# Two staging buffers for token-major Q and K, their stores in the sync queue, and turned blocks moved into the next tile

## Chip, cores, metric

One core of one Trainium2 chip. The metric is device microseconds of one execution of the program. A difference is called faster or slower from 2% on, and below that it is given with its interval.

## The reference, cut to what matters

Forward and backward of a small transformer block: a recurrent attention with memory, then a gated FFN. The part that matters here is the forward recurrence over 64 segments of 32 tokens. Each segment attends over 8 memory rows and its own 32 tokens, and its output gives the memory rows of the next segment, so the segments are a chain:

```python
for s in range(n_seg):
    h = concatenate([mem, xs], axis=1)
    q, k, v = h @ Wq, h @ Wk, h @ Wv
    p = softmax(where(mask, q @ k.T * scale, -1e9))
    o = (p @ v) @ Wo
    mem = o[:, :M, :]          # the next segment needs this
    outs.append(o[:, M:, :])
```

The rest (FFN, backward recurrence, weight gradients) comes after the chain and reads what the chain saved: Q and K by token (T1; the T0 blocks hold those of the memory rows), V, the attention output by token (X_o), its projection by rows (Oh), the weights turned, that is transposed on their way by the DMA (Td, To, Tg, Tu, Tq, Tk, Tv).

## The kernel before

A tile is four segments; r is the segment's place in it, jm its place among sixteen. The chain's instructions have a high priority. Everything else in a segment is side work on the sync queue (SP) and on GpSimd (POOL): turned transfers through two staging buffers, and their stores.

```python
qk_st = A(15, 2, 2, 512)                       # one buffer for token-major Q and K
stg_b = [A(36 + 4 * i, 2048) for i in range(2)]  # two staging buffers

def stg():                                     # next staging buffer, in turn
    rot[0] += 1
    for fn in unsaved.pop(rot[0] % 2, ()): fn()   # its last content is stored first
    return stg_b[rot[0] % 2]
def save(*pairs):                              # a store from GpSimd, put off
    ... nc.gpsimd.dma_start(out=out, in_=in_) ...
def piece():                                   # turn one of 44 pieces of weights
    T, ot = dr["T" + nm], stg()
    nc.sync.dma_start_transpose(out=..., in_=Ws[...]); save((T[...], ot))
...
        with k.prio.crit():                    # the chain
            ...
            qk_turned(s, 0)
            for w, nm in enumerate("qk"):
                nc.scalar.dma_start(out=dr["T1" + nm][s], in_=qk_st[:, w]...)
            ...
        nc.gpsimd.dma_start(out=dr["P_all"][s], ...)
        for g in range(2):
            nc.sync.dma_start(out=dr["VG"][s, ...], in_=Vs[...])
        rest_rows(s + 1)                       # GpSimd copies that the next scores need
        nc.gpsimd.tensor_copy(out=mblk[:, :, jm * M:(jm + 1) * M], in_=orr)   # frees orr
        if due and jm % 3 == 0 and jm > 0:
            residual(n, h_t, x2_t, to_v)       # VectorE; rows fetched at jm % 3 == 1
        save_all()
        if r == 1:  ... T0 block: stg, transpose, save
        if r < 3 and s >= 4:
            piece()
        if jm == 15: ... orow = projection of the memory block, stored to Oh
        if r == 3:
            to_token_major(xblk, t, at)        # both halves of a tile, X_o
        if jm == 15:
            to_token_major(mblk, ...)          # two more, and one for mh
```

The tool that builds the program takes the order of each engine's instructions from the data dependencies and its priorities. The order of the text is not the order of issue.

Of the kernel before, what the change touches and what calls it, by code (L numbers as in the profile page):

```python
# [10 lines left out]
BF16 = mybir.dt.bfloat16  # L11
# [4 lines left out]
P = 128  # L16
# [129 lines left out]
def run_all(k: _K):  # L146
    nc, tc, ctx = k.nc, k.tc, k.ctx
    S, D, M, H, Dh, HD, F = k.S, k.D, k.M, k.H, k.Dh, k.HD, k.F
    SEG, L, NSEG, NT, KC, DP, MC, DC, FC = k.SEG, k.L, k.NSEG, k.NT, k.KC, k.DP, k.MC, k.DC, k.FC
# [25 lines left out]
    ident = const.tile([P, P], BF16)  # L175
# [28 lines left out]
    def dt(name, shape, dtype=BF16):  # L204
        return dram.tile(shape, dtype, name=name)
# [3 lines left out]
    dr = dict(XN=dt("XN", [NB * P, DP]), Hh=dt("Hh", [S, D]), HN=dt("HN", [S, D]), DH=dt("DH", [S, D], FP32),  # L209
              DHb=dt("DHb", [NB * P, DP]), Zt=dt("Zt", [S, F]), DGP=dt("DGP", [S, F]), DU=dt("DU", [S, F]),  # L210
              VG=dt("VG", [NSEG, 2 * L, W2]), XR=dt("XR", [NT * 32, DP]), P_all=dt("P_all", [NSEG, P, 8 * L]),
              X_o=dt("X_o", [NB, P, MC * P]), HC=dt("HC", [NB * P, DP]), Oh=dt("Oh", [S, D]))
# [2 lines left out]
        dr["M_" + nm] = dt("M_" + nm, [NT, P, MC * 32])  # L215
    for nm in ("q", "k", "v"):
        dr["T" + nm] = dt("T" + nm, [P, MC, D])
    for nm in ("q", "k"):
        dr["T1" + nm] = dt("T1" + nm, [NSEG, P, 1024])
        dr["T0" + nm] = dt("T0" + nm, [NSEG // 8, P, W2])  # L220
    dr["To"] = dt("To", [P, KC, HD])
    dr["Td"] = dt("Td", [P, KC, F])
# [127 lines left out]
def forward_chain(k: _K):  # L350
    nc, tc = k.nc, k.tc
    S, D, M, H, Dh, HD = k.S, k.D, k.M, k.H, k.Dh, k.HD
    SEG, L, NSEG, NT, KC, DP, MC, DC = k.SEG, k.L, k.NSEG, k.NT, k.KC, k.DP, k.MC, k.DC
    X2 = k.aps["A_x"][0]
    MEM0 = k.aps["A_mem0"][0]
    ident, dr, sel, maskb = k.ident, k.dr, k.sel, k.maskb
    smal = k._small
    W, A, B = k.W, k.A, k.B
# [5 lines left out]
    HB = 4  # L364
    qT_b = [A(2.5 * i, 32, L) for i in range(2)]
    kT_b = [A(5 + 2.5 * i, 32, L) for i in range(2)]
    V_b = [A(11, 2048), W(92, 2048)]
    qk_st = A(15, 2, 2, 512)
    hR_b = [A(19 + 0.5 * i, KC, 64) for i in range(2)]
    R_b = [[W(56 + 4 * i, 32, 64) for i in range(2)], [A(20 + 4 * i, 32, 64) for i in range(2)]]  # L370
    stg_b = [A(36 + 4 * i, 2048) for i in range(2)]
    xblk_b = [A(52 - 24 * i, 32, P) for i in range(2)]
    mblk = A(44, 32, P)
# [4 lines left out]
    or_b = [B(1.25 + 0.5 * i, 32, M) for i in range(3)]  # L378
    x2_t, h_t = B(2.75, D), B(3.625, D)
    hx = B(4.5, KC, P)  # L380
    orow = B(6.25, D)
    P_b = [B(7.125 + 0.625 * i, 8, L) for i in range(2)]
    mh = B(8.375, KC, P)
    om_b = [B(9.375 + 0.5 * i, 256) for i in range(2)]
    maskt = B(10.375, HB * L)

    nc.gpsimd.memset(hT_flat[:, :, NWIN * L:], 0.0)
    nc.gpsimd.memset(PT_bd, 0.0)
    om = k.f32("f1", 256, "om")
    pO = k.po1()  # L390
    nc.vector.memset(pO[:], 0.0)
    nc.vector.tensor_copy(out=maskt.rearrange("p (h n) -> p h n", n=L), in_=maskb[:].unsqueeze(1).to_broadcast([P, HB, L]))
# [101 lines left out]
    def stg():  # L494
        rot[0] += 1
        for fn in unsaved.pop(rot[0] % 2, ()):
            fn()
        return stg_b[rot[0] % 2]

    def save(*pairs):  # L500
        def fn():
            for out, in_ in pairs:
                nc.gpsimd.dma_start(out=out, in_=in_)
        unsaved[rot[0] % 2] = [fn]

    def save_all():
        for i in (1, 2):
            for fn in unsaved.pop((rot[0] + i) % 2, ()):
                fn()
# [5 lines left out]
    def qk_rows(s, b):  # L515
        sl = s % NWIN
        banks = [k.ps1(), k.ps1()]
        for w in range(2):
            for kc in range(KC - 1):
                for q in range(4):  # L520
                    nc.tensor.matmul(banks[w][32 * q:32 * q + 32, :], lhsT=hT_roll[:, kc, sl, M:L], rhs=(Wq_sb, Wk_sb)[w][:, kc, col(q, b)],  # L521
                                     start=(kc == 0), stop=False, skip_group_check=True)
        for q in range(4):
            for w in range(2):
                last = nc.tensor.matmul(banks[w][32 * q:32 * q + 32, :], lhsT=hT_roll[64 * w:64 * w + 64, KC - 1, sl, M:L],
                                        rhs=Wqk3[64 * w:64 * w + 64, col(q, b)], start=False, stop=True, skip_group_check=True)
        for w in range(2):
            k.evac(qk_st[:, w, b, :], banks[w][:], "vs"[w])
        return last

    def qk_turned(s, b):
        pt = k.ps1()[:].bitcast(BF16)
        for w in range(2):
            for i in range(4):
                nc.tensor.transpose(pt[:, w * 512 + i * P:w * 512 + (i + 1) * P], qk_st[:, w, b, i * P:(i + 1) * P], ident[:, :])
        for w, dst in ((0, qT_b[s % 2]), (1, kT_b[s % 2])):
            k.evac(dst[:, 16 * b:16 * b + 16, M:L], pt[:, w * 512:(w + 1) * 512].rearrange("p (c n) -> p c n", n=32), "vs"[w])

    def to_token_major(blk, t, ins=None):
        for hf in range(2):  # L540
            ot = stg()
            with tc.issue_after(ins) if ins is not None else nullcontext():
                nc.sync.dma_start_transpose(out=ot.rearrange("p (a b) -> p a b", b=P),
                                            in_=blk[:, 16 * hf:16 * hf + 16, :].rearrange("p c n -> p (c n)"))
            save((dr["X_o"][t][:, hf * 2048:(hf + 1) * 2048], ot))

    pieces = []
    for nm, Ws in (("d", k.aps["B_w_down"]), ("o", k.Wo2)):
# [6 lines left out]
    def piece():  # L555
        if not pieces:
            return
        nm, Ws, i0, n = pieces.pop(0)
        T, ot = dr["T" + nm], stg()
        if nm in "do":  # L560
            o4 = ot.rearrange("p (c n) -> p c n", c=KC)
            nc.sync.dma_start_transpose(out=o4[:, 0:3, 0:n], in_=Ws[i0:i0 + n, 0:3 * P])
            nc.sync.dma_start_transpose(out=o4[:, 3, 0:n], in_=Ws[i0:i0 + n, D - P:D])
            save((T[:, 0:3, i0:i0 + n], o4[:, 0:3, 0:n]), (T[0:64, 3, i0:i0 + n], o4[64:P, 3, 0:n]))
        else:
            m = n // P
            o3 = ot[:, 0:m * D].rearrange("p (c d) -> p c d", d=D)
            nc.sync.dma_start_transpose(out=o3, in_=Ws[:, i0:i0 + n])
            save((T[:, i0 // P:i0 // P + m, :], o3))
# [18 lines left out]
    for s in range(NSEG):  # L588
        t, r = divmod(s, 4)
        jm = s % 16  # L590
# [3 lines left out]
        xblk, om2 = xblk_b[t % 2], om_b[s % 2]  # L594
        end = s == NSEG - 1
        if due and jm % 3 == 1:
            fetch(due[0], h_t, x2_t)
        with k.prio.crit():
# [86 lines left out]
                k.fl.at(0)  # L685
                k.fl.at(1)
            qk_turned(s, 0)
            for w, nm in enumerate("qk"):
                nc.scalar.dma_start(out=dr["T1" + nm][s], in_=qk_st[:, w].rearrange("p b n -> p (b n)"))
            value_rows(0)  # L690
            pS0 = scores(0)
            softmax(0, pS0)
# [34 lines left out]
        nc.gpsimd.dma_start(out=oh[s, M:SEG, 0:256], in_=om2[0:24, :])  # L727
        nc.gpsimd.dma_start(out=oh[s, M:SEG, 256:D], in_=om2[32:56, 0:D - 256])
        nc.gpsimd.dma_start(out=dr["P_all"][s], in_=P_sb.rearrange("p h n -> p (h n)"))
        for g in range(2):  # L730
            nc.sync.dma_start(out=dr["VG"][s, L * g:L * g + L], in_=Vs[64 * g:64 * g + L, :])
        if not end:
# [7 lines left out]
        if due and jm % 3 == 0 and jm > 0:  # L740
            n = due.pop(0)
            residual(n, h_t, x2_t, to_v)
        save_all()
        if (r == 0 and t > 0) or s == 2:
            prep_tile(t + 2)
        if r == 1:
            w = bu // 4
            ot = stg()
            nc.sync.dma_start_transpose(out=ot.rearrange("p (a b) -> p a b", b=P), in_=R_b[bm % 2][w].rearrange("p c n -> p (c n)"))
            save((dr["T0" + "qk"[w]][bm], ot))  # L750
        if r < 3 and s >= 4:
            piece()
        at = None
        if jm == 15:
            px = k.fx1()
# [4 lines left out]
            due = list(range(t - 3, t + 1))  # L760
            if end:
                at = k.fl.at(3).ins
        if r == 3:
            to_token_major(xblk, t, at)
        if jm == 15:
            to_token_major(mblk, NT + s // 16, at)
            mrow = stg()
            nc.sync.dma_start_transpose(out=mrow[:, 0:DP].rearrange("p (a b) -> p a b", b=P),
                                        in_=mh.rearrange("p c n -> p (c n)"))
            r0 = (NT + s // 16) * P  # L770
            save((dr["XN"][r0:r0 + P, :], mrow[:, 0:DP]))
    save_all()
    assert not pieces and due == list(range(NT - 4, NT))
    late = [(B(0, D), B(0.875, D)), (W(61.5, D), W(62.375, D))]
# [178 lines left out]
def backward_chain(k: _K):  # L953
    nc, tc = k.nc, k.tc
# [37 lines left out]
    def load_seg(s):  # L992
        if s < NSEG - 1:
            load_v(s)
        for nm, T_sb in (("q", Q_sb), ("k", K_sb)):
            t1 = dr["T1" + nm][s].rearrange("(g x i) n -> g i x n", g=2, x=2)
            t0 = dr["T0" + nm][s // 8].rearrange("(x s i) (g n) -> s g i x n", x=2, s=8, g=2)
            for g in range(2):
                for src, i0, i1 in ((t1[g], M, L), (t0[s % 8, g], 0, M)):
                    nc.sync.dma_start(out=T_sb[64 * g + i0:64 * g + i1].rearrange("p (x c) n -> p x (c n)", x=2), in_=src)  # L1000
        P_sb = Pb[s % 2]
        nc.gpsimd.dma_start(out=P_sb.rearrange("p h n -> p (h n)"), in_=dr["P_all"][s])
        for g in range(2):
            pool_op = nc.gpsimd.tensor_copy(out=P_bd[64 * g:64 * g + L, :, g, :], in_=P_sb[64 * g:64 * g + L, :, :])
        stores("mid", s, pool_op.ins)
# [419 lines left out]
```

## Time and profile before

| | before |
|---|---|
| median | 3188.19 us (four runs, 3183.85 to 3195.59; 3185.03 of three at the time of the prediction) |
| span of the profiled run | 3196.7 us, mean granted clock 0.974 (an execution of 3198.43 us, not among the four) |
| forward chain, end of segment 0 to end of segment 62 | 998.4 us |
| a clean segment | 15.09 us |

A segment's end is the end of the VectorE copy that writes the next memory rows. A segment's length is the difference of two such ends, so lengths can be compared one by one between kernels. In the views PE is TensorE, PEld its weight loads, DVE VectorE, ACT ScalarE, POOL GpSimd; a q at the end (SPq, ACTq) marks issues of transfers in that engine's queue. arA, arB and arW are on-chip buffers, psf, po and fx the accumulators that matmuls write; the chain's copies out of them are called evictions. One more view: GpSimd's timeline at the end of segment 19. The columns are the start, the time, engine, line, operation, tiles, count and, in brackets, the idle time before and what ended it.

```profile
374.52 0.51 POOL L727 DMA_DIRECT2D Oh<-arB  x1 [4.32 <-DVE arB L713]
375.02 1.08 POOL L739 COPY arA<-arB 128x256 bf16<-128x256 bf16 x3
376.05 0.56 POOL L759 DMA_DIRECT2D Oh<-arB  x1
...
379.66 0.55 POOL L503 DMA_DIRECT2D X_o<-arA  x1 [2.00 <-DMA arA<-arA]
```

### The profile page before, as it was taken

What the parts mean: (1) busy time and instruction counts of PE and PEld (TensorE: products, weight loads), DVE (VectorE), ACT (ScalarE), POOL (GpSimd) and SP (SyncE); (2) the same over time, 40 slices, a digit from 0 to 9 for tenths busy, and PEclk for the clock granted to TensorE, in tenths of its full rate; (3) what the DMA queues carried; (4) which work ended last, traced back from release to release, by engine and by line L of the source; (5) the groups of instructions that cost most, each with busy time, mean ns of one, the idle gap of its engine ahead of it and who ended that gap; (6) DMA issues with size and microseconds to landing.
All of it is one profiled execution on the core that took longest, in us unless ns stands there. A gap on an engine that the chain in (4) does not pass through costs nothing.

```text
span 3196.7 us, 107765 instructions
## 1 busy us (share of the span) xinstructions
PE 2924.5 (91%) x47442; PEld 1776.2 (56%) x47442; DVE 1364.9 (43%) x3433; ACT 1057.8 (33%) x2501; POOL 723.7 (23%) x1648
## 2 busy tenths in 40 slices
PE   6899899989988869977999999999999699999998
PEld 3455455555544547645666666666666454444444
DVE  4455455455455567753444544445444201111110
ACT  2444344344434323322333333333433101110210
POOL 2232332223232221121112211112211111111111
PEclk9999999999999979988999999999999899999999
DMA  6968765867667888894454555445545898959952
GB/s 237 198 152 177 181 163 141 194 162 183 167 155 192 246 207 195 191 274 147 132 138 137 132 149 134 140 132 140 144 134 141 266 269 226 198 181 195 191 147 72
DMA packets 757305, 556.21 MB, mean 174 GB/s; under 512 B 627732, under 2 KB 656388, under 8 KB 754404
## 3 DMA queue, kind: packets, MB, share of 16 engines
q1 hardware_dynamic: 671828, 294.81, 44.2%
q0 software_dynamic: 66576, 220.95, 20.3%
q10 hardware_dynamic: 18432, 33.56, 3.1%
q8 instruction: 372, 6.09, 0.8%
q14 instruction: 97, 0.79, 0.1%
HBM read 167.32 MB, written 234.23 MB: 126 GB/s over the span
## 4 chain that ended last, share of the span: by engine, by line
PE 69%; DMA 10%; DVE 9%; issue 7%; ACT 3%; SPq 2%; POOL 1%; ACTq 0%; POOLq 0%; DVEq 0%
PE psf L1286 8%; PE po L1120 7%; PE psf L1071 7%; PE psf L633 5%; PE psf L521 4%; PE psf L1048 4%; PE psf L1307 4%; PE po L678 3%; PE fx L1184 3%; PE psf L847 2%; DVE arA L75 2%; PE fx L454 2%; PE fx L937 2%; PE fx L1291 2%; PE psf L1142 2%
## 5 line engine op out<-in xcount | busy, mean ns | idle before, releaser
L75 DVE CAST arA<-psf 128x256 bf16<-128x256 f32 (+4 forms) x997 | 470.8, 492 | 920.1 <-PE psf L1286 258.9
L76 ACT CAST arA<-psf 128x384 bf16<-128x384 f32 (+6 forms) x979 | 390.0, 420 | 1179.8 <-PE psf L1286 256.5
L1120 PE MATMUL po<-arW,arA 128*32 128x448 bf16 x6144 | 348.9, 357 | 22.8 <-DVE arA L75 20.5
L633 PE MATMUL psf<-arW,arA 128*64 128x512 bf16 x1536 | 253.3, 393 | 0.0
L1286 PE MATMUL psf<-arW,arA 128*128 128x512 bf16 x1000 | 252.0, 379 | 0.0
L1071 PEld LDWEIGHTS <-arW 128*128 128x128 bf16 x8192 | 214.1, 96 | 27.5 <-issue 27.5
L1120 PEld LDWEIGHTS <-arA 128*32 128x32 bf16 x6144 | 152.1, 97 | 135.9 <-DVE arA L75 21.7
L1286 PEld LDWEIGHTS <-arA 128*128 128x128 bf16 x1440 | 136.0, 98 | 164.8 <-issue 13.8
L1071 PE MATMUL psf<-arA,arW 128*128 128x40 bf16 x8192 | 217.7, 180 | 8.4 <-DVE arA L1146 5.1
L521 PE MATMUL psf<-arW,arA 128*32 128x512 bf16 x3072 | 193.9, 385 | 12.5 <-DVE arA L722 12.5
L847 PE MATMUL psf<-arW 128*128 128x256 bf16 x1344 | 159.3, 281 | 45.1 <-DMA arW<-arW 34.3
L847 PEld LDWEIGHTS <-arW 128*128 128x128 bf16 x1344 | 134.9, 101 | 71.5 <-DMA arW<-arW 29.1
L678 PE MATMUL po<-arW,arA 128*32 128x256 bf16 (+1 forms) x4096 | 142.4, 265 | 9.8 <-DVE arA L75 6.8
L1048 PEld LDWEIGHTS <-arW 128*128 128x128 bf16 x2048 | 87.6, 100 | 89.6 <-issue 62.9
L1048 PE MATMUL psf<-arB,arW 128*128 128x80 bf16 x2048 | 98.1, 202 | 41.4 <-DMA arW<-T0k 22.6
L454 PE MATMUL fx<-arA,arW 128*128 128x64 bf16 (+1 forms) x2048 | 84.8, 196 | 43.2 <-ACT arB L76 30.7
L1081 ACT COPY arA<-psf 128x1024 bf16<-128x1024 bf16 x128 | 123.3, 1015 | 2.3 <-PE psf L1080 0.4
L521 PEld LDWEIGHTS <-arA 128*32 128x32 bf16 x3072 | 70.5, 96 | 90.1 <-DVE arA L722 18.1
L76 ACT COPY arA<-psf 128x512 bf16<-128x512 bf16 (+2 forms) x136 | 79.0, 582 | 111.5 <-DVE arA L75 87.9
L678 PEld LDWEIGHTS <-arA 128*32 128x32 bf16 x4096 | 94.6, 97 | 30.2 <-DVE arA L75 10.2
L633 PEld LDWEIGHTS <-arA 128*64 128x64 bf16 x1536 | 85.0, 111 | 44.1 <-issue 1.4
L454 PEld LDWEIGHTS <-arW 128*128 128x128 bf16 (+1 forms) x2048 | 71.2, 99 | 65.4 <-issue 43.8
(285 smaller groups left out, 4618.6 us busy)
## 6 DMA issues: line engine op xcount, KB each, us to landing
X_o<-arA POOLq DMA_DIRECT2D x40, 512.0 KB, 4.1
T1k<-arA ACTq DMA_DIRECT2D x64, 256.0 KB
T1q<-arA ACTq DMA_DIRECT2D x64, 256.0 KB
arW<-T1q SPq DMA_DIRECT2D x128, 128.0 KB
arW<-T1k SPq DMA_DIRECT2D x128, 128.0 KB
X_v<-arA POOLq DMA_DIRECT2D x32, 512.0 KB, 5.3
X_k<-arA POOLq DMA_DIRECT2D x32, 512.0 KB, 3.8
X_q<-arA POOLq DMA_DIRECT2D x32, 512.0 KB, 3.6
```

What stands on the lines that cost most here:

```text
L75: return nc.vector.tensor_copy(out=out, in_=in_)
L76: return nc.scalar.copy(out=out, in_=in_)
L454: nc.tensor.matmul(banks[w][:, i * 64:(i + 1) * 64], lhsT=lhsT, rhs=xr[lo:hi, kc, :], start=(kc == 0 and i == 0), stop=(kc == KC - 1), ski ...
L521: nc.tensor.matmul(banks[w][32 * q:32 * q + 32, :], lhsT=hT_roll[:, kc, sl, M:L], rhs=(Wq_sb, Wk_sb)[w][:, kc, col(q, b)], start=(kc == 0) ...
L633: nc.tensor.matmul(pV[b][64 * g:64 * g + 64, 0:512], lhsT=hT_flat[:, kc, sl * L:sl * L + 64], rhs=Wv_sb[:, kc, n * 512:(n + 1) * 512], sta ...
L678: nc.tensor.matmul(pO[32 * q:32 * q + 32, 0:w], lhsT=xblk[:, j, r * SEG:(r + 1) * SEG], rhs=Wo_sb[:, cj(j), 256 * dh:256 * dh + w], start= ...
L847: nc.tensor.matmul(ps[:, f2 * 256:(f2 + 1) * 256], lhsT=Wt[:, kc, c * P:(c + 1) * P], rhs=xT[:, kc, :], start=(kc == 0), stop=(kc == KC - 1))
L1048: nc.tensor.matmul(ps[b][:, i * 2 * L:(i + 1) * 2 * L], lhsT=lhs[:, at, :], rhs=rhs_bd[:, cl // 2, :, :].rearrange("p g n -> p (g n)"), st ...
L1071: nc.tensor.matmul(pss[b][:, jj * L:(jj + 1) * L], lhsT=WoT_sb[:, kc, c * P:(c + 1) * P], rhs=do_roll[:, kc, sl, :], start=(kc == 0), stop ...
L1120: nc.tensor.matmul(pH[32 * (j % 4):32 * (j % 4) + 32, 0:D], lhsT=blk[nm][:, j, r * SEG:(r + 1) * SEG], rhs=WT[:, cj(j), :], start=(nm == " ...
L1286: nc.tensor.matmul(pa[2 * kc + g][:, 0:w], lhsT=lhs_of(b)[:, kc * P:(kc + 1) * P], rhs=rhs_of(b, g), start=(b == 0), stop=(b == nblk - 1), ...
L1307: nc.tensor.matmul(pa[i][:, 0:D], lhsT=lhs_of(b, i), rhs=rhs_of(b), start=(bi == 0), stop=(bi == len(nblk) - 1))
```

## The change

Its intent: take the stores of Q and K out of ScalarE's queue, where they can stand in front of the chain's copies, and thin out the turned transfers at the end of each tile and of each sixteenth segment.

```diff
-    qk_st = A(15, 2, 2, 512)
+    qk_st = [[A(15, 2, 512), A(17, 2, 512)], [<two other places>]]
-    orow = B(6.25, D)
+    orow = x2_t                                # to make room
@@ chain
-            for w, nm in enumerate("qk"):
-                nc.scalar.dma_start(out=dr["T1" + nm][s], in_=qk_st[:, w]...)
@@ after the chain
+        for w in range(2):
+            nc.sync.dma_start(out=dr["T1"][s, :, w], in_=qk_st[s % 2][w]...)
@@ side work
-        if r == 1:
+        if s >= 4 and ((r > 0 and jm < 15) or (jm == 0)):
+            piece()
+        if r == 2:
             ... T0 block
-        if r < 3 and s >= 4:
-            piece()
-        if r == 3:
-            to_token_major(xblk, t, at)
         if jm == 15: ... two halves of mblk, mh
+        if t > 0 and r < 2:
+            to_token_major(xblk_b[(t - 1) % 2], t - 1, r)   # one half each
```

(Cut: moved places of small buffers, the loads of T1 in the backward chain, the last tile.)

More of the change, by code (lines that the diff above doesn't have):

```diff
@@ L217, in run_all @@
         dr["T" + nm] = dt("T" + nm, [P, MC, D])
+    dr["T1"] = dt("T1", [NSEG, P, 2, 1024])
     for nm in ("q", "k"):
-        dr["T1" + nm] = dt("T1" + nm, [NSEG, P, 1024])
         dr["T0" + nm] = dt("T0" + nm, [NSEG // 8, P, W2])
@@ L367, in forward_chain @@
     V_b = [A(11, 2048), W(92, 2048)]
-    qk_st = A(15, 2, 2, 512)
+    qk_st = [[A(15, 2, 512), A(17, 2, 512)],
+             [k.f32("f1", 512, "q_st")[:].bitcast(BF16).rearrange("p (b n) -> p b n", b=2), B(8.75, 2, 512)]]
     hR_b = [A(19 + 0.5 * i, KC, 64) for i in range(2)]
@@ L380, in forward_chain @@
     hx = B(4.5, KC, P)
-    orow = B(6.25, D)
-    P_b = [B(7.125 + 0.625 * i, 8, L) for i in range(2)]
-    mh = B(8.375, KC, P)
-    om_b = [B(9.375 + 0.5 * i, 256) for i in range(2)]
-    maskt = B(10.375, HB * L)
+    orow = x2_t
+    P_b = [B(5.5 + 0.625 * i, 8, L) for i in range(2)]
+    mh = B(6.75, KC, P)
+    om_b = [B(7.75 + 0.5 * i, 256) for i in range(2)]
+    maskt = A(64, HB * L)
     nc.gpsimd.memset(hT_flat[:, :, NWIN * L:], 0.0)
     nc.gpsimd.memset(PT_bd, 0.0)
-    om = k.f32("f1", 256, "om")
+    om = k.f32("f3", 256, "om")
     pO = k.po1()
@@ L527, in qk_rows @@
         for w in range(2):
-            k.evac(qk_st[:, w, b, :], banks[w][:], "vs"[w])
+            k.evac(qk_st[s % 2][w][:, b, :], banks[w][:], "vs"[w])
         return last
@@ L534, in qk_turned, with to_token_major @@
             for i in range(4):
-                nc.tensor.transpose(pt[:, w * 512 + i * P:w * 512 + (i + 1) * P], qk_st[:, w, b, i * P:(i + 1) * P], ident[:, :])
+                nc.tensor.transpose(pt[:, w * 512 + i * P:w * 512 + (i + 1) * P], qk_st[s % 2][w][:, b, i * P:(i + 1) * P], ident[:, :])
         for w, dst in ((0, qT_b[s % 2]), (1, kT_b[s % 2])):
             k.evac(dst[:, 16 * b:16 * b + 16, M:L], pt[:, w * 512:(w + 1) * 512].rearrange("p (c n) -> p c n", n=32), "vs"[w])
-    def to_token_major(blk, t, ins=None):
-        for hf in range(2):
-            ot = stg()
-            with tc.issue_after(ins) if ins is not None else nullcontext():
-                nc.sync.dma_start_transpose(out=ot.rearrange("p (a b) -> p a b", b=P),
-                                            in_=blk[:, 16 * hf:16 * hf + 16, :].rearrange("p c n -> p (c n)"))
-            save((dr["X_o"][t][:, hf * 2048:(hf + 1) * 2048], ot))
+    def to_token_major(blk, t, hf, ins=None):
+        ot = stg()
+        with tc.issue_after(ins) if ins is not None else nullcontext():
+            nc.sync.dma_start_transpose(out=ot.rearrange("p (a b) -> p a b", b=P),
+                                        in_=blk[:, 16 * hf:16 * hf + 16, :].rearrange("p c n -> p (c n)"))
+        save((dr["X_o"][t][:, hf * 2048:(hf + 1) * 2048], ot))
     pieces = []
@@ L687, in forward_chain @@
             qk_turned(s, 0)
-            for w, nm in enumerate("qk"):
-                nc.scalar.dma_start(out=dr["T1" + nm][s], in_=qk_st[:, w].rearrange("p b n -> p (b n)"))
             value_rows(0)
@@ L729, in forward_chain @@
         nc.gpsimd.dma_start(out=dr["P_all"][s], in_=P_sb.rearrange("p h n -> p (h n)"))
+        for w in range(2):
+            nc.sync.dma_start(out=dr["T1"][s, :, w], in_=qk_st[s % 2][w].rearrange("p b n -> p (b n)"))
         for g in range(2):
@@ L762, in forward_chain @@
                 at = k.fl.at(3).ins
-        if r == 3:
-            to_token_major(xblk, t, at)
         if jm == 15:
-            to_token_major(mblk, NT + s // 16, at)
+            for hf in range(2):
+                to_token_major(mblk, NT + s // 16, hf, at)
             mrow = stg()
@@ L771, in forward_chain @@
             save((dr["XN"][r0:r0 + P, :], mrow[:, 0:DP]))
+        if t > 0 and r < 2:
+            to_token_major(xblk_b[(t - 1) % 2], t - 1, r)
+        if end:
+            for hf in range(2):
+                to_token_major(xblk, t, hf, at)
     save_all()
@@ L994, in load_seg @@
             load_v(s)
-        for nm, T_sb in (("q", Q_sb), ("k", K_sb)):
-            t1 = dr["T1" + nm][s].rearrange("(g x i) n -> g i x n", g=2, x=2)
+        for w, (nm, T_sb) in enumerate((("q", Q_sb), ("k", K_sb))):
+            t1 = dr["T1"][s, :, w].rearrange("(g x i) n -> g i x n", g=2, x=2)
             t0 = dr["T0" + nm][s // 8].rearrange("(x s i) (g n) -> s g i x n", x=2, s=8, g=2)
```

## The prediction

> **What bounds the kernel now.** I read the page first, then the granted clock, then the lengths of the 64 forward segments, then the waits and the timelines inside the segments that are too long. The page says TensorE is the bound and that the chain that ended last lies mostly on it:
>
> ```profile
> PE 2924.5 (91%) x47442; PEld 1776.2 (56%) x47442; DVE 1364.9 (43%) x3433; ACT 1057.8 (33%) x2501; POOL 723.7 (23%) x1648
> PE 69%; DMA 10%; DVE 9%; issue 7%; ACT 3%; SPq 2%; POOL 1%; ACTq 0%; POOLq 0%; DVEq 0%
> ```
>
> The 10% on DMA is what matters here: in a recurrent chain a transfer should not stand on the path. The change touches only the forward chain, which runs to about 1070 us of 3197. I took the end of each segment from the copy that writes the next memory rows (DVE, L722). Undisturbed segments take 15.09 us, over and over. Nearly all exceptions follow the start (segments 4 to 6) and each sixteenth segment (16 to 20, 32 to 36, 48 to 53). The windows of single segments show a clean one, two of the long ones (17 and 18), and for comparison segment 34, which is long only because a quarter of the extra output projection (L757, 32 matmuls per sixteen segments) is threaded into it:
>
> ```profile
> core 0: us, PE busy (x) PEld busy (x) DVE busy (x) ACT busy (x) POOL busy (x), PEclk, DMA share, GB/s
> 285.22:300.31 15.09, 14.17 (x279) 8.15 (x280) 7.94 (x24) 6.76 (x17) 3.92 (x12) 1.00 0.34 82
> 316.32:337.53 21.21, 18.06 (x288) 9.71 (x287) 7.82 (x25) 6.65 (x17) 5.96 (x14) 0.92 0.86 198
> 337.53:358.78 21.25, 17.94 (x288) 9.66 (x287) 7.92 (x25) 6.87 (x17) 8.01 (x20) 0.92 0.73 183
> ...
> 597.36:613.79 16.43, 16.39 (x288) 9.20 (x287) 7.82 (x24) 6.76 (x17) 3.07 (x8) 1.00 0.94 231
> ```
>
> Segments 17 and 18 hold the same 288 matmuls as segment 34 and take 4.8 us more each; TensorE is idle for over 3 us in each. ScalarE's timeline of segment 17 shows why. ACTq lines are issues in ScalarE's own queue:
>
> ```profile
> 320.75 0.59 ACT L76 CAST arA<-psf 128x512 bf16<-128x512 f32 x1 [1.16 <-PE psf L525]
> 325.05 0.33 ACTq L689 DMA_DIRECT2D T1k<-arA  x1
> 325.42 0.58 ACT L76 COPY arA<-psf 128x512 bf16<-128x512 bf16 x1 [4.08 <-DMA arA<-arB]
> 326.90 0.33 ACTq L689 DMA_DIRECT2D T1q<-arA  x1
> ```
>
> The store of K could not be issued for 3.7 us after the copy before it, and the copy of turned K, which the scores need, stood behind it. What ended the wait is a turned transfer of the sync queue (arA<-arB, L768) that has no data in common with the store. The records of the semaphores explain it: sync and scalar DMAs together post to eight semaphores in turn, and a new DMA waits until the earlier user of its semaphore has landed. When the sync queue is jammed with turned blocks, this reuse reaches over to ScalarE. The table of waits, over 100 to 1060 us, lists all of this:
>
> ```profile
> ACT arA L76 <- DMA arA<-arB: 8.8, 3, 4.1
> ACT arA L76 <- DMA arA<-in_B_w_down_dram: 4.4, 1, 4.4
> ACT arA L76 <- DMA arA<-in_A_Wo_dram: 4.1, 1, 4.1
> ACT arA L76 <- DMA VG<-arA: 1.7, 1, 1.7
> ACT arA L76 <- DMA arA<-arA: 1.1, 1, 1.1
> ```
>
> The second kind of stall, in segments 20, 36 and 52, is another one: VectorE waits at the residual (L576) for a row fetched back from Oh.
>
> ```profile
> DVE arB L576 <- DMA arB<-Oh: 16.3, 3, 6.2
> ```
>
> **What the Trainium skill says.** "DMA: Bandwidth & Descriptors", § Why a DMA increments its semaphore by 16 and not by 1: each transfer in flight should have its own semaphore. The trace agrees with the consequence: with eight in rotation, T1k waited 3.7 us for an unrelated one. The same page, § Rules for kernel authors: a transpose beside ordinary DMAs needs no wait; so the wait is not one that the data or the hardware asks for. § Issuing engines are not separate DMA queues: changing the issuing engine saves only sequencer time. So I expect no bandwidth from the move; what it saves is only that ScalarE's in-order queue no longer holds the wait. "Perfetto Trace Analysis", § Summary: the profiler window per engine type: a hardware-queue DMA is shown from the end of its semaphore wait on. The trace agrees: T1k is 0.33 us long although it held the queue for 3.7 us.
>
> **The change, part by part.**
>
> (a) T1 stores leave ScalarE. The waits above sum to 8.8 + 4.4 + 4.1 + 1.7 + 1.1 = 20.1 us over 8 places. In a clean segment the same copy is idle for 0.44 us (it waits for VectorE), so 8 x 0.44 = 3.5 is not the store's: 16.6 us. By segment lengths: segment 5 is 21.84 and about 16.7 without it (15.09 and one extra unit of rest rows, 1.3, and some of segment 6's 0.8): 5.1; segments 17 and 18, 4.8 each; 33 (17.62 against 16.44 of 34) 1.2; 49 (17.94) 1.5; 9, 0.3. Sum 17.7, and these are on the path, as the scores' matmuls wait for the copy. I take **17 us**. In the clean segments the move gives nothing: the store's 0.33 us ends where the copy is released by VectorE anyway (274.79 against 274.84 us).
>
> (b) The second staging buffer. With the stores issued after the chain, one buffer would make the next segment's evictions wait for their landing; two leave a whole segment of 15 us. It removes no wait that I see now; it pays for (a). Expected: 0.
>
> (c) Turned blocks. Now both halves of a tile go out in the tile's last segment, and at each sixteenth segment with two of the memory block and one more: five uses of two staging buffers, with a store's landing (4 to 5 us) between uses. After: three there, two in segments 16, 17 and 18. That is the jam in which (a)'s waits arise; with (a) alone most of the time is gone already, so the two overlap. Its own gain would be at segments 20, 36, 52: two turned halves of 3.8 us each now run across the Oh store and its fetch (376.1 to 386.3 us: landing 5.3, then 4.4). At the medians of the page and DMA view (3.0 to 3.5 each) that is some 2 to 3 us sooner, three times. Against it: the row for Oh now shares its buffer with the fetched x row, so the x fetch too comes after the store, some 0.5 us each. Net **+3 us**, the least certain term.
>
> (d) The sync queue gets 128 issues of 0.33 to 0.40 us, 0.7 us per 15 us segment, beside about 9 us of its own at worst. No cost in the chain. But around 1070 to 1124 us, at the start of the FFN, the sync queue itself is on the chain that ended last; two more issues there: **-1 us**.
>
> (e) Backward loads read the same bytes in the same 2 KB runs, from one tensor: 0. Moved mask and rows: 0.
>
> Sum: 17 + 3 - 1 = 19 us; 3185 - 19 = 3166 us.
>
> **The rivals.**
>
> Rival 1, another wait takes its place: GpSimd is in order too, and waits for turned blocks before its stores (X_o <- DMA arA<-arA, 106.5 us in all); the copies of the rest rows for the next scores stand in that queue. In segment 5 they end at 134.98 us, 2 us later than the scores would like. For it: the same jam feeds both. Against: the jam is smaller after (c). If half of (a) comes back: gain 8 to 10, 3176 us.
>
> Rival 2, the spreading does more: the stalls at segments 20, 36 and 52 vanish whole. Their excess is 7.5 + 8.2 + 6.9 = 22.6 us (with the clock that falls to 0.85 there). For: the collision with the two turned halves is plain. Against: the Oh store is late mainly because the threaded projection ends only in segment 19, which the change does not move. Then 3185 - 17 - 22 = 3146 us.
>
> Rival 3, the sync queue becomes the bound: stores late behind turned blocks hold the staging buffers and the value stores, evictions of two segments later wait. Against: the queue idles half of a clean segment (it waits 14 us at a time for the value copies). If so, or if instructions are reordered to a bad place: 3185 or some us more.
>
> **Range and chances.** All rivals lie within 1.3% of the time before, and 2% would take 64 us, more than all stalls of the forward chain together (17.7 + 22.6, about 40). So within 2% is nearly sure. The range goes from the lower part of rival 2 to no gain: 3152 to 3182.
>
> **What would show each step right or wrong.** (a): no ACT wait for a DMA left in the forward chain, segments 5, 17, 18 at about 16.5 us. Wrong if these segments stay over 18 us with another releaser. (b): no eviction that waits for a T1 landing. (c): the residual's wait of 16.3 us falls to about 10; if it stays or grows, the projection's place rules it. (d): sync queue issues at the FFN start shifted by 1 us. The prediction fails as a whole if the reordered instructions make a new regular wait of even 0.3 us in each of the 64 segments, which would eat the gain.

## More of the kernel before

L739 copies three segments' memory columns into the memory block; they had to wait until the projection of the last sixteen segments had read the block (374.5 us), and they run at once after it. L503 is the one line of all staging stores.

## The result

| | before | after |
|---|---|---|
| median of four runs | 3188.19 us | 3287.05 us (3279.12 to 3292.33) |
| ratio | | 1.0306, 95% interval 1.0273 to 1.0338: slower |
| profiled span, clock | 3196.7, 0.974 | 3281.2, 0.961 |
| forward chain, segments 1 to 62 | 998.4 us | 1086.4 us |
| from there to the end | 2139.1 us | 2136.1 us |

A ratio compares the fast runs of two kernels measured in the same rounds, so it is not quite the ratio of the medians. In the profiles the loss lies whole in the forward chain. They differ by 84.5 us and the medians by 98.9, as the profiled execution of before lies 10 us above its median and that of after 4 us below.

The first lines of the page show no more work, only more waiting; the share of DMA in the chain that ended last has grown from 10% to 12%:

```profile
PE 2923.6 (89%) x47432; PEld 1763.4 (54%) x47442; DVE 1369.3 (42%) x3433; ACT 1059.3 (32%) x2501; POOL 727.0 (22%) x1648
PE 66%; DMA 12%; DVE 8%; issue 7%; ACT 3%; SPq 2%; POOL 1%; ACTq 0%; POOLq 0%; DVEq 0%
```

The lengths of the segments (us) tell where. All others are alike within 0.8 us:

| segment | 5 | 17 | 18 | 33 | 49 | 8 | 20 | 36 | 52 |
|---|---|---|---|---|---|---|---|---|---|
| before | 21.84 | 21.21 | 21.25 | 17.62 | 17.94 | 15.09 | 22.61 | 23.27 | 21.95 |
| after | 15.79 | 16.53 | 16.53 | 16.53 | 16.53 | 33.44 | 53.31 | 49.33 | 51.86 |

The first five lose 17.9 us together, the last four gain 105.0. The windows of segments 17, 8 and 20 of the changed kernel (columns as in the windows of before):

```profile
328.02:344.55 16.53, 16.51 (x288) 8.92 (x287) 7.92 (x25) 6.76 (x17) 4.24 (x9) 1.00 0.94 191
173.41:206.85 33.44, 15.64 (x278) 8.42 (x278) 8.26 (x24) 6.87 (x17) 10.60 (x26) 0.74 0.63 156
377.54:430.85 53.31, 20.35 (x291) 10.79 (x286) 9.70 (x30) 7.46 (x20) 15.59 (x39) 0.62 0.80 181
```

Segment 17 is now nearly all matmul. Segment 8 holds the 278 matmuls of a clean segment and is longer by 18 us; segment 20 has 39 GpSimd instructions where segment 17 has 9. Who is waited for, over 100 to 1050 us, as line, releaser, total, times, longest:

```profile
ACT arB L76 <- POOL arA L739: 83.2, 3, 29.4
DVE arB L75 <- POOL arA L739: 77.8, 3, 27.5
DVE arB L576 <- DMA arB<-in_A_x_dram: 17.1, 3, 8.3
PE psf L609 <- POOL arA L466: 16.8, 1, 16.8
```

None of ScalarE's waits for a DMA is left. In their place ScalarE and VectorE wait for GpSimd's copies into the memory block (L739: until it is done, the buffer orr of three segments before can't be written), and TensorE once for its copies of the rest rows (L466). GpSimd's timeline in segment 20 shows what stood in front of them (L504 is now the line of all staging stores):

```profile
380.28 0.55 POOL L504 DMA_DIRECT2D Tg<-arA  x1 [7.50 <-DMA arA<-in_B_w_gate_dram]
...
387.70 0.56 POOL L504 DMA_DIRECT2D Tg<-arA  x1 [5.10 <-DMA arA<-in_B_w_gate_dram]
394.19 0.55 POOL L504 DMA_DIRECT2D Tg<-arA  x1 [5.93 <-DMA arA<-in_B_w_gate_dram]
...
401.11 0.54 POOL L504 DMA_DIRECT2D Tu<-arA  x1 [3.88 <-DMA arA<-in_B_w_up_dram]
401.64 0.52 POOL L725 DMA_DIRECT2D Oh<-arB  x1
402.16 1.08 POOL L739 COPY arA<-arB 128x256 bf16<-128x256 bf16 x3
```

And TensorE over the same time:

```profile
377.93 0.83 PE L522 MATMUL psf<-arW,arA 128*32 128x512 bf16 x12
402.86 1.47 PE L522 MATMUL psf<-arW,arA 128*32 128x512 bf16 x12 [24.10 <-ACT arB L76]
```

By the program's text the three pieces Tg of 380 to 394 us belong to segments 22, 23 and 25, and Tu to segment 26. They are stored at the turn from segment 19 to 20, each after a turned transfer that itself waited for the store before it, some 7 us a round. L739, which before ran at 375 us, runs at 402.

So the order has changed. I counted the staging stores on GpSimd in both traces by the number of segments whose mh copy (another copy of memory columns, one per segment) came before them:

```
count   before                       after
18      To To T0q To To To To        To To X_o To To T0q To To
19      -                            Tg Tg
20      -                            Tg Tg Tu
21      X_o X_o Tg T0k Tg            X_o Tu X_o Tu
22      Tg                           T0k Tu
25      X_o X_o Tg T0q Tu            X_o X_o
26      Tu                           T0q
29      X_o X_o Tu T0k Tu            X_o X_o
30      Tq                           T0k
```

Before, pieces are spread over the segments. After, they lie in bunches behind segments 5, 16, 32 and 48, with none in between. The long segments are those into which the bunches reach.

**My theory.** The staging buffers are used in turn. Within a tile the uses were P, T P, P, X X (P a piece of weights, T the T0 block, X a half of X_o): both buffers hold an X once per tile, and an X must wait for the chain. After the change they are X, P X, P T, P: strictly other, P, other, P. All pieces fall on one buffer and everything that depends on the chain falls on the other. Nothing then holds the pieces to their segments except three uses in a row at each sixteenth segment, which shift the turn. The tool queues them as early as it can, and GpSimd, in order, stands at their stores while the chain's copies wait behind. (That the three uses at each sixteenth segment are what ends a bunch fits the counts; no run tests it.)

**Rivals.** First: the stores of Q and K, now in the sync queue, delay the turned transfers. Second: the buffer that orow and x2_t now share delays the fetched rows. Third: the turned halves, now just after a sixteenth segment, collide there with the other transfers.

### The profile page after: what moved, and what is told of

The parts are those of the page before. It is cut to its first block, busy times and chain, and to the rows that moved or that the text cites. A ratio compares the mean times of both kernels' runs of the same rounds, so it can differ in the third digit from the quotient of the medians.

```text
span 3281.2 us, 108027 instructions
## 1 busy us (share of the span) xinstructions
PE 2923.6 (89%) x47432; PEld 1763.4 (54%) x47442; DVE 1369.3 (42%) x3433; ACT 1059.3 (32%) x2501; POOL 727.0 (22%) x1648
## 3 DMA queue, kind: packets, MB, share of 16 engines
q0 software_dynamic: 66576, 220.95, 19.8%
## 4 chain that ended last, share of the span: by engine, by line
PE 66%; DMA 12%; DVE 8%; issue 7%; ACT 3%; SPq 2%; POOL 1%; ACTq 0%; POOLq 0%; DVEq 0%
PE psf L1290 8%; PE po L1124 7%; PE psf L1075 6%; PE psf L522 4%; PE psf L633 4%; PE psf L1052 4%; PE psf L1311 3%; PE po L678 3%; PE fx L1188 3%; PE psf L851 2%; DVE arA L75 2%; PE fx L941 2%; PE fx L1295 2%; PE psf L1146 2%; PE fx L455 2%
## 5 line engine op out<-in xcount | busy, mean ns | idle before, releaser
L75 DVE CAST arA<-psf 128x256 bf16<-128x256 f32 (+3 forms) x933 | 427.2, 480 | 823.7 <-PE psf L1290 258.9
L76 ACT CAST arA<-psf 128x96 bf16<-128x96 f32 (+5 forms) x915 | 352.9, 409 | 1084.3 <-PE psf L1290 256.5
L633 PE MATMUL psf<-arW,arA 128*64 128x512 bf16 x1536 | 222.3, 390 | 0.0
L76 ACT CAST arB<-psf 128x64 bf16<-128x64 f32 (+3 forms) x384 | 121.9, 318 | 223.2 <-PE psf L526 108.1
L75 DVE CAST arB<-psf 128x64 bf16<-128x64 f32 (+2 forms) x256 | 73.4, 288 | 77.8 <-POOL arA L739 77.8
```

What stands on the lines that cost most here:

```text
L75: return nc.vector.tensor_copy(out=out, in_=in_)
L76: return nc.scalar.copy(out=out, in_=in_)
L633: nc.tensor.matmul(pV[b][64 * g:64 * g + 64, 0:512], lhsT=hT_flat[:, kc, sl * L:sl * L + 64], rhs=Wv_sb[:, kc, n * 512:(n + 1) * 512], sta ...
```

## Experiments

Segment lengths are from the profiled run of each kernel, in us; "forward" is the end of segment 0 to the end of segment 62 (before 998.4, after 1086.4).

### Each half of the change alone

**Stores alone**: the changed kernel with the side work as before.

```diff
-        if s >= 4 and ((r > 0 and jm < 15) or (jm == 0)): piece()
-        if r == 2:  ... T0
+        if r == 1:  ... T0
+        if r < 3 and s >= 4: piece()
+        if r == 3: both halves of xblk
-        if t > 0 and r < 2: one half of the tile before
```

> The changed kernel with the turned blocks put back where they were (both halves of a tile in its last segment, pieces in segments 0 to 2 of a tile, rest rows in segment 1); the stores of token-major Q and K stay in the sync queue with two buffers. Theory (the pieces of weights to be turned got a staging buffer to themselves by strict alternation, were queued far ahead, and GpSimd waits in order for them): the four long segments 8, 20, 36 and 52 (33, 53, 49, 52 us in the changed kernel) are gone, segments 5, 17, 18, 33, 49 keep their gain of some 18 us; about 3170 us, ratio to before 0.994. Rival 1 (the stores in the sync queue delay the turned blocks and thereby GpSimd): the long segments stay, 3250 us or more. Rival 2 (the shared row buffer for Oh and x): the excess of segments 20, 36, 52 stays above 25 us each.

Measured: 3179.94 us (six runs), ratio 0.9981 (0.9953 to 1.0009), forward 983.3. No segment is long as in the changed kernel: segment 8 is 15.01; segments 20, 36, 52 are 22.87, 26.23, 21.40. Segments 5, 17, 18, 33, 49 keep the gain (15.84, 16.52, 16.53, 16.52, 16.52). The first rival falls. The second does as the cause of the loss, since this kernel shares the buffer too; segment 36, at 26.23, is 3 us worse than before, and to that I return. The time alone cannot tell this gain from none; the profile's forward part is 15 us shorter.

**Blocks alone**: the kernel before with only the turned blocks, the pieces and T0 at their new places.

```diff
-    def to_token_major(blk, t, ins=None): both halves
+    def to_token_major(blk, t, hf, ins=None): one half
+        if s >= 4 and ((r > 0 and jm < 15) or (jm == 0)): piece()
+        if r == 2: ... T0
+        if t > 0 and r < 2: to_token_major(xblk_b[(t - 1) % 2], t - 1, r)
```

> The kernel before with only the turned blocks moved (halves in the first two segments of the next tile, pieces and rest rows at their new places); stores of Q and K stay on ScalarE with one buffer, no buffer moved. Its program has the same bunched order of GpSimd's staging stores as the changed kernel. Theory: the four long segments appear, some 105 us, and ScalarE's waits for turned transfers (16 us or more) stay on top: 3280 to 3330 us, ratio 1.03 to 1.045. Rival 1 (stores in the sync queue are the cause) and rival 2 (shared row buffer): about 3190 us, no segment above 25 us.

Measured: 3291.1 us, ratio 1.0328 (1.0292 to 1.0364), forward 1095.2. The waits, over 100 to 1050 us (L738 is here the copy into the memory block):

```profile
ACT arB L76 <- POOL arA L738: 62.5, 3, 21.8
ACT arA L76 <- DMA arA<-arA: 13.3, 3, 6.7
```

A loss of the same size comes with the turned blocks alone, so the first two rivals are out. It is not made up as I expected, though. Segments 8, 20, 36 and 52 (24.12, 45.64, 41.38, 45.63) gain 74 us, not 105. Segments 7, 19, 33 and 50 are 6 to 8 us longer each, 28.5 together, and in each of them ScalarE waits for a turned transfer: here its queue still holds the stores, and its waits for DMAs sum to 33.5 us against 20.1 before.

### The same work, only the order mended

**Block before piece**: one swap in the changed kernel, in the tile's second segment. The uses become X, X P, P T, P.

```diff
+        if t > 0 and r == 1:
+            to_token_major(xblk_b[(t - 1) % 2], t - 1, r)
         if s >= 4 and ((r > 0 and jm < 15) or (jm == 0)):
             piece()
-        if t > 0 and r < 2:
+        if t > 0 and r == 0:
```

> The changed kernel with one swap: in the second segment of a tile the turned half block is queued before the piece of weights, not after it. The work is the same; the uses of the two staging buffers are no longer strictly piece, other, piece, other, so pieces wait for blocks. Theory: pieces are spread over the segments again, the long segments 8, 20, 36, 52 fall below 25 us each; 3165 to 3180 us, ratio 0.993 to 0.998. Rivals (stores in the sync queue, shared row buffer, collision of turned blocks with the Oh fetch in the first segments after a sixteenth): all of that is still there, so about 3285 us.

Measured: 3188.72 us, ratio 1.0006 (0.9976 to 1.0035), forward 986.2. Segments 8, 20, 36, 52: 15.01, 22.34, 27.81, 20.70. The 98 us are gone with a swap of two calls. My 25 us were exceeded in segment 36, and the time is no better than before, above the 3165 to 3180 us that I had expected, although the forward part is 12 us shorter in the profile. The third rival is out as the cause of the long segments: the halves are still in the tile's first two segments.

**Pieces in place**: the alternation is kept, but each piece is queued behind its own segment's value store.

```diff
-            nc.sync.dma_start(out=dr["VG"][s, ...], in_=Vs[...])
+            vg = nc.sync.dma_start(out=dr["VG"][s, ...], in_=Vs[...])
-            piece()
+            with tc.issue_after(vg.ins):       # order of issue on the sync queue
+                piece()
```

> The changed kernel with the strict alternation of buffers kept, but each piece's transfers are queued behind the value store of their own segment in the sync queue (an order of issue only, no wait). Theory (the run-ahead is the cause, the alternation only allows it): no long segment, each segment has one piece; 3160 to 3175 us, ratio 0.992 to 0.996, at least as good as the swap. If the alternation itself or the load of the queues were the cause: still above 3250 us.

Measured: 3189.5 us, ratio 1.0002 (0.9974 to 1.003), forward 990.4; segments 8, 20, 36, 52: 15.78, 26.16, 25.70, 21.49. The time is again above the range that I gave, but the question is answered: the alternation does no harm when the pieces are held to their segments. What does the harm is the run-ahead that it allows.

### The fault made on purpose

**Own buffer**: the kernel before, nothing moved, but pieces stage in buffer 0 and all others in buffer 1.

```diff
-    def stg():
-        rot[0] += 1
+    def stg(own=1):
+        rot[0] = own
-        T, ot = dr["T" + nm], stg()
+        T, ot = dr["T" + nm], stg(0)
```

> The kernel before, nothing moved, but the pieces of weights stage in buffer 0 alone and all other turned blocks in buffer 1. This makes on purpose the state that the theory blames. In the built program GpSimd's piece stores are bunched: all 44 pieces are queued by segment 24. Theory: long segments appear where the bunches lie (between 6 and 24), none after 25 beyond the known 36 and 52; 50 to 200 us slower, 3240 to 3390 us. Rival (the place of the turned halves in the next tile or the sync queue's load is the cause): about 3190 us, since neither is changed.

Measured: 3294.27 us, ratio 1.0347 (1.0325 to 1.0368), forward 1099.0. The long segments lie between 6 and 24, where the bunches are: 7 is 24.14, 8 is 33.69, 12 is 29.39, 16 is 34.10, 20 is 43.93, 24 is 22.95. From segment 25 on, when no piece is left, the lengths are those of before or shorter (segment 36 is 22.69, 52 is 21.65; only 57 and 61 are longer, by 0.4 and 0.7), although all other blocks still share one buffer. So the run-ahead alone, with no transfer moved to another segment of the text, costs 100 us. But that this is about the changed kernel's loss is in part chance, as the waits show (100 to 1100 us):

```profile
ACT arB L76 <- POOL arA L739: 23.7, 3, 20.4
PE fx L757 <- POOL arA L739: 15.6, 1, 15.6
ACT arA L76 <- DMA VG<-arW: 13.9, 1, 13.9
ACT arA L76 <- DMA arA<-in_A_Wo_dram: 8.7, 1, 8.7
```

Only segments 16, 20 and 24 (47 us over before) are held by GpSimd's copies. Segments 6, 7, 8, 10, 12, 15 and 19 (66 us over) are held by ScalarE's waits for DMAs, 61.6 us in all against 20.1 before: the stores of Q and K are still in its queue, and these waits end with landings of the sync queue's transfers. One fault, two in-order queues that pay for it.

### Which queue holds the chain

**Piece stores in the sync queue**: the changed kernel, with the stores of the pieces taken from GpSimd.

```diff
-    def save(*pairs):
+    def save(*pairs, eng=nc.gpsimd):
...
+            save(<a piece>, eng=nc.sync)
```

> The changed kernel with only the stores of the turned pieces of weights taken from GpSimd's queue to the sync queue. In the built program the pieces are bunched as in the changed kernel (eight before segment 9, and again after 16, 32 and 48), so the run-ahead and its transfers stay; what goes is that GpSimd waits for them in order. Theory (the long segments come from GpSimd standing at piece stores with the copies of rest rows and of the memory block behind them): no wait of TensorE, ScalarE or VectorE of over 5 us for a GpSimd copy, segment 8 near 15 us, segments 20, 36, 52 at 21 to 28 us (the residual's wait is left); 3170 to 3200 us. Rival (the bunched transfers themselves or the sync queue's lag hold the chain): long segments stay or return with value stores or staging buffers as the releaser, above 3250 us.

Measured: 3236.74 us, ratio 1.0148 (1.0115 to 1.0181), forward 1045.2. Segment 8 is 15.02. Segments 20, 36, 52 are 40.30, 41.09, 42.20, much over the 21 to 28 that I expected, and the time lies between the 3200 us at most of my theory and the 3250 us at least of its rival. The waits (100 to 1100 us):

```profile
DVE arB L576 <- DMA arB<-in_A_x_dram: 70.2, 3, 23.9
ACT arB L76 <- POOL arA L739: 5.1, 3, 1.7
```

No engine waits long for a GpSimd copy any more, so that half of the theory holds. But the residual now waits up to 23.9 us for its fetched rows. The waits inside segment 20 (375 to 415 us) show why:

```profile
POOL X_o L504 <- DMA arA<-arA: 20.9, 1, 20.9
```

GpSimd stood at the store of a turned half block, whose transfer was itself late behind the bunched pieces in the sync queue, and the fetch for the residual stood behind it. So the bunch can harm by two ways: GpSimd in order at the pieces' own stores, and the sync queue in order at the pieces' transfers and stores, with GpSimd in order behind. With the first taken away half of the loss is left. This does not split the changed kernel's loss between the two, since the edit also puts 44 pieces' stores, each behind a wait for its own transfer, into the sync queue; in the changed kernel the residual waited 17.1 us, not 70.2. One more thing shows here alone: in segment 10 (19.62) an eviction waits 6.6 us for the landing of a Q or K store (T<-arA).

### The residual

What is left in segments 20, 36 and 52 is the wait of VectorE at L576: the residual, which adds rows of Oh to rows of x, both fetched back. **Late residual** fetches the rows and adds the residual one segment later. I put it on stores-alone, on the kernel before, on the swap and on pieces in place:

```diff
-        if due and jm % 3 == 1:               # fetch
+        if due and jm % 3 == 2:
-        if due and jm % 3 == 0 and jm > 0:    # residual
+        if due and jm % 3 == 1 and jm > 1:
```

> Stores-alone kernel with the residual of a fetched row block one segment later: fetch at the third, residual at the second following segment (2 and 4, 5 and 7, ... of sixteen instead of 1 and 3, 4 and 6). Theory (the wait of VectorE at the residual in segments 20, 36, 52 comes only from the late projection, store and fetch in a row, each excess of 6 to 11 us being this wait): these segments fall to about 15.5 us, no wait of the residual for a DMA; 20 to 25 us below stores-alone, 3155 us, ratio 0.988 to 0.992. Rival (another transfer or copy is just as late there, so the wait only changes its name): within 8 us of stores-alone.

> The kernel before with the same shift of the residual alone. Theory: minus 20 us (segments 20, 36, 52 from 22 to about 16 us), segments 5, 17, 18, 33, 49 as before: about 3165 us, ratio 0.994. Rival: no change, ratio 1.0.

> The changed kernel with the half block queued before the piece and with the residual one segment later: the whole intent of the change without its two faults. Theory: segments 20, 36 and 52 fall to about 15.5 us as with stores-alone and late residual; 3150 to 3165 us, ratio 0.988 to 0.994; if the move of the turned blocks gives anything once nothing else is in the way, it beats stores-alone with late residual (ratio 0.9912), else the two are equal within 0.3%.

> The changed kernel with each piece queued behind its segment's value store and with the residual one segment later. Theory: as the swap with late residual, 3150 to 3165 us, all segments after the first eight below 17 us.

| kernel with late residual | median | ratio to before (95%) | forward | segments 20, 36, 52 |
|---|---|---|---|---|
| stores alone | 3155.56 | 0.9912 (0.9893 to 0.9931) | 958.8 | 15.41, 15.41, 15.41 |
| before | 3172.95 | 0.9964 (0.9946 to 0.9982) | 981.7 | 15.44, 15.43, 15.44 |
| block before piece | 3162.38 | 0.9912 (0.9888 to 0.9935) | 967.8 | 15.41, 15.40, 15.41 |
| pieces in place | 3160.83 | 0.9912 (0.9887 to 0.9938) | 960.3 | 15.40, 15.40, 15.53 |

The stall is gone in all four. Three further readings. First, with this noise removed, the stores' move shows in the times too: 0.9912 against 0.9964, with intervals that do not overlap, is 0.5%, some 17 us (more on this under (a)). Second, the moved blocks add nothing: both mended versions come to the ratio of stores alone. Third, the kernel before with the late residual keeps ScalarE's waits (its segments 17 and 18 are 20.45 and 20.28; 5.5 us at arA<-arB alone), as it should. It gained less than the 20 us that I expected (0.9964 against 0.994): in its profile segments 3 and 58 are 4.3 and 5.0 us longer than before, and TensorE stands there for 3.8 and 3.3 us with no releaser that the profile shows. Stores alone with the late residual is the shortest kernel of this case by its interval, though its 0.9% under before is less than the 2% from which a change is called faster. The segments of pieces in place are below 17 us after the first eight, as expected; in the swap two are not quite (19 is 17.51, 51 is 19.18).

**Own row**: stores alone with a buffer for orow again, to see what the shared one costs.

```diff
-    orow = x2_t
+    orow = A(10, D)
```

> Stores-alone kernel in which the row for Oh has a buffer of its own again (a free place), not that of the fetched x row. Theory (the shared buffer makes the x fetch, the second of two, wait for the store, so that the residual waits for x: 19.8 us against 16.3 before): the residual waits for Oh again, 15 to 17 us in all, 3 to 4 us less than stores-alone in the span; not resolvable in the times. Rival: the wait stays at about 20 us with Oh in the place of x.

Measured: 3181.52 us, ratio 0.9983 (0.9958 to 1.0007). The residual's wait is for Oh again, and it is 15.5 us against 19.8 us in stores alone:

```profile
DVE arB L576 <- DMA arB<-Oh: 15.5, 3, 5.9
```

So the sharing costs 4.3 us in all, 1.4 us on average. The segments show it uneven: 36 is 22.53 here against 26.23, while 20 and 52 differ by 0.5 us or less. As expected, the times do not resolve it.

## Why the prediction was wrong, point by point

**(a) was right, in mechanism and size.** I said 17 us from segments 5, 17, 18, 33 and 49. They lost 17.9 in the changed kernel, and no wait of ScalarE for a DMA stayed. (I counted eight places where the table has seven: 20.1 less 7 x 0.44 is 17.0, not 16.6.) The times give some 17 us too where the residual is out of the way, but there the agreement may be luck: between the two profiles of that pair these five segments differ by 10.4 us only, and segments 3, 4 and 58 by another 10.5. Clean segments became shorter by 0.07 us, nothing as I had said, except the last seven: 15.01 us against 14.75. There the scores stand before the value rows in TensorE's order; I did not test that.

**(b) was right**: no eviction of note waits for a T1 landing in the changed kernel (with the pieces' stores in the sync queue, one does, 6.6 us).

**(c) is the step that failed.** It said that fewer uses of the staging buffers per segment mean a smaller jam, +3 us. I counted uses per segment and took them to stay in their segments. I did not follow which of the two buffers each use falls on, though the text of the kernel has all that is needed for it. The runs show -105 us in four segments in place of +3: blocks alone loses as much in total, the swap brings it back, and a buffer for the pieces alone makes a loss of that size without any move, if partly through ScalarE's queue. The smaller part of (c) failed too: the collision of turned halves with the Oh fetch was to give 2 to 3 us three times, but the residual waits 19.1 us with the halves moved (block before piece) and 19.8 with them in place (stores alone). The cost of the shared buffer was mis-sized: 0.5 us each was said, 1.4 on average was measured.

**(d)**: I took 1 us off at the start of the FFN; from segment 62 to the end the changed kernel is 3 us shorter in the profile, so no such cost shows, in spans that vary by several us.

**(e)**: nothing contradicts it; it was not tested by itself.

**The rivals.** Rival 1 named the queue that did the harm, GpSimd in order, but held that it would shrink after (c). It named the rest rows as what stands behind; that is so in segment 8 alone (16.8 us), while in 20, 36 and 52 it was the copy into the memory block. The 134.98 us that it gives for the end of the rest rows' copies is the end of just that copy (L739); theirs (L465) ended at 134.64. Rival 3 ended with "instructions are reordered to a bad place" and gave it "3185 or some us more". That was the right direction, and the size was not worked out: one round of turned transfer and store is 7 us in this trace (380.28, 387.70, 394.19, 401.11), and four of them in front of a chain copy are 28. The sentence that all stalls of the forward chain together are less than 2%, so that slower by 2% is nearly excluded, holds only for gains: it bounds what can be taken away, not what a new order can add. And the last sign of failure looked for a small new wait in each of the 64 segments; what came were four large ones.

**What stays open.** The swap and pieces in place are 12 and 8 us shorter than before in the forward part of the profile, yet equal in time (ratios 1.0006 and 1.0002). Each interval is about 0.3% wide on either side, 9 us, so a gain of that size may be hidden; I do not know whether it is. Nor are single profiles a firm measure: from segment 62 to the end, those of block before piece and of own buffer differ by 12 us (2132.4 and 2144.1).

## What to carry to other kernels

With a ring of buffers, write down for each buffer the sequence of its users: if a change gives one buffer only users that depend on nothing, the program's builder may queue them all at once, and every in-order queue behind them pays. Hold such side work to its place with an order of issue, or mix it with users that wait for the chain. And an upper bound from the stalls that can be removed says nothing of the stalls that a change can add.

## What the Trainium skill lacked or had wrong

- "DMA: Bandwidth & Descriptors", § Issuing engines are not separate DMA queues, says that issuing from several engines saves only the sequencer's time, usually small. Here the choice of the queue was worth far more by what stands behind the issue: 17.9 us for 128 stores of 0.33 to 0.40 us moved from ScalarE to the sync queue, and about half of the loss for the pieces' stores moved from GpSimd (1.0148 against 1.0306). The section leaves out what it costs when an issue waits and holds the queue behind it.
- The same page, § Why a DMA increments its semaphore by 16 and not by 1, asks for one semaphore per transfer in flight. It does not give the price of reusing eight in turn: a store waited 3.7 us here for an unrelated turned transfer.
- "Advanced Engine Details and Errata", § X-Bar Transpose (TRN2), has turned transfers as fast as regular ones. In the chain that ended last of the kernel before, turned blocks within on-chip memory took 6.4 to 7.6 us from issue to landing (at 560.87 and 816.55 us), against a median of 4.1 us for the store of the same half block (X_o). The issue alone held the sync queue for 3.7 us in the median of the 40 turned half blocks (L543), where a store of Q or K held ScalarE's for 0.33 to 0.40. The transfers were not alone in the queues, so this is no measure of the peak.
- No page that I read tells that a buffer ring decides how far side work can run ahead of a chain: 105 us in four segments.
